# Delta-rule attention and an MLP mixer on one core: 180 steps of a written order of issue moved

## The chip, the cores and the metric

The kernel runs on one core of one Trainium2 chip. A core has five engines that take their instructions in order, each from its own queue: TensorE (PE in the profile), VectorE (DVE), ScalarE (ACT), GpSimd (POOL) and SyncE (SP), which here issues all the DMA transfers. The metric is the device time of one execution in microseconds (us); less is better.

## The reference

Two blocks follow each other. Each of 4 batches and 8 heads runs a delta rule over 768 positions with a 48x48 state, and the joined heads (768 rows of 384) pass a token mixer and a channel mixer:

```python
for t in range(S):                       # S = 768, per batch and head
    kt, vt, bt = k_n[:, :, t], v[:, :, t], beta[:, :, t, None]     # k_n: k over its norm
    y[:, :, t] = einsum('bhd,bhde->bhe', q[:, :, t], state)
    v_old = einsum('bhde,bhd->bhe', state, kt)
    state = state + bt * einsum('bhd,bhe->bhde', kt, vt - v_old)
xt = x.transpose(0, 2, 1)                # x: y with the heads side by side
h = maximum(xt @ w_tok1, 0) @ w_tok2     # 768 -> 256 -> 768
u = x + h.transpose(0, 2, 1)
out = u + maximum(u @ w_ch1, 0) @ w_ch2  # 384 -> 1536 -> 384
```

## The kernel before

The recurrence is computed in chunks. All work is cut into jobs, Python generators in which each `next` issues one step. A string, `order`, names the job whose next step is issued; the launch loop walks through it:

```python
for word in order.split():
    name, _, n = word.partition("*")
    for _ in range(int(n or 1)):
        next(jobs[name])
```

Nothing is reordered after that: each engine runs its instructions in this order, and waits for what an instruction needs. So the string sets, for each queue, what stands behind what. In all there are 2610 steps. The jobs, by letter, with the lines that matter:

- `w0` to `w33` load and round pieces of the weights: a DMA of 384 KB or 256 KB (L280), two ACT steps (L286, L287), a shift on DVE (L289), an addition on POOL (L293).
- `k` loads keys and queries of a unit (128 rows of one batch's chunk pair), `p` prepares it: squares on ACT (L539), norms on DVE and ACT, transposes on PE (L562, L582) with ACT copies, the scaled mask `mb` (L574, on POOL from the fourth unit on) and scaled keys (L592). `c` and `d` form gram matrices on PE (L511) and mask them into `gm` on DVE (L517).
- `t` hands quarters of a unit's `gm` to an inversion: for the first six units by copies on ACT (L674), DVE (L677) and POOL (L679), later by four DMA writes to `n_dram` (L686). `i` inverts for several units at once, a chain on DVE: a transpose (L731) or a read of `n_dram` (L733), then for each row a product (L747) and an addition (L751); in the early rounds, at the end, a transpose (L757), an ACT and a DVE scaling (L758, L759). `f` brings the parts back (for later rounds by DMA from `w_dram`, L711).
- `h` (first six units only) and `j` join the inverted parts: PE products `p_z` (L781) and `p_x` (L794, L888), ACT copies (L799). The first `h` also fills a tile `z` with zeros on POOL (L619).
- `r` is the recurrence: `r0` to `r23` for the first two batches, `r24` to `r35` for the last two together, a serial chain through PE (L1013, L1038, L1042, L1056, L1059), DVE (L1022, L1070) and ACT (L1047, L1076, L1081), with a DMA of the output rows (L1083) and `l` to read them back (L1095).
- `m0`, `m1` are the mixers of the first two batches; `T2` is the token part of the third (L1227, six groups of PE matmuls, one per chunk, then L1242), `T3` of the fourth; `A`, `F`, `B` are the channel parts of the last two; `W`, `S`, `s` are sums of weights for them.
- `x`, `z` and `Y` issue matmuls on zeros whose result nobody reads (128x128 and 128x512 columns at L235, 64x128 at L245).

`order` begins with the weights, keys and warm matmuls, passes the six early units (inversion rounds 0 and 1), the writes of the third round's units, and from there mixes the recurrence with `m0` and `m1`. The line of `order` with `w22*4 t9*3` and the lines with `r34` and `T2` are those that the third and fourth places below belong to.

Of the kernel before, what the change touches and what calls it, by code (L numbers as in the profile page):

```python
# [23 lines left out]
def kernel(  # L24
# [1761 lines left out]
    h0 h1 h0 w8*2 h1 Y i0 f0 Y p4 f1 h2*2 p5*3 f0*2 w6 h0*5 k6*5 p6 z f2*2 k8*3 p5
    w6 p5 p3 p5 j0*3 f1*2 h1*5 j0*2 w8*2 w17 f2 h2*3 v0 t4*2 w17 r0*5 p6 h2*2 c5*2
    v1 w11*2 j1 p5 k7*2 c5 k7 c5 r0 c5 r0*2 w14*2 v1 w11*2 k7*2 p7 d5*5 r1*5 w14*2
    p6*2 t5 j1 t5*2 r1*2 j1 j2 p7 h3*2 r1*3 p6*3 i1*2 r2*5 k8*2 f3*2 w9 k9*3 j1*2
    v2*2 i1*3 j2*2 r2*2 f3 i1*2 p6*3 w16 v2 w16*3 r2*2 h3 r2 i1 d6 r3*5 i1*2 w9*3  # L1790
    v2 d6 h3 v2 w0 h3*2 r3 h3 d6*2 w0 d6 j3 c6*5 r3*4 w0 j2 w0 p8*2 j2 r4 p8 r4*4
    k9*3 j3*2 r4*2 i1*2 w24 i1*2 p7*7 r4 c7 r4 r5*5 k10 p9 k10 p9 c7 r4 c7*3 i1
    w5*2 p7 r5*2 w24*3 r5*3 j3*2 i1 r6*4 w26 v3*5 p9 k11 r6 d7*5 w26*3 p8*3 t6*2
    r6*2 w5*2 p8*4 v4*2 t6 i1 r6*3 h5*2 h4*2 k10*2 f4*3 c8*2 k10 p10 w28*2 c8*2 r7
    c8 r7*3 d8*4 p9 d8 w28 h4*5 p9 t6 r7*2 j4 w28 p9*3 r7*2 p9 w7 d9 w7 v4*2 f5*2
    w27*2 w7*2 d9*4 c9*2 f5 c9*3 t7*2 t8 r7*2 t7*2 j4*2 v4 p10*2 h5 r8*3 w29 t8*3
    w29 w27*2 r8*2 w29*2 q3 w29 j4*2 r8 w22*4 t9*3 r8*3 p9 r9 p10 r9*3 t9 v5 h5*3
    j5 i2 r9 w4*2 r8 h5 i2*5 w4 i2 w19*2 k10 w32 p10*2 w32 v7 k12 m0*2 k11 k12 q0
    v5*3 p10*2 r9*2 j5*2 k11*3 i2*2 r9 w4 i2 j5 i2*3 p10 v5 r9*2 d10*3 r10 v7*2 j5
    i2*2 r10*4 w12 i2 k12 i2*2 m0 w32 k11 k12 w32 r10*2 m0 p11 k12*4 w19 p11 r10  # L1800
    c10 r10 c10 r10 w33 d10*2 q2 Y r11*4 v7 r11*3 w19 c10 q1 w30 c10 r11 k12*2
    i2*3 r11 v6*4 i2*5 m0*3 i2*5 q5 i2 m0 p11*4 c10 p11 m0 p11*2 m0*2 k12*2 w12
    m0*3 v6 f6*3 w12 d11 c11*2 d11*2 c11 w33 c11 d11*2 j6 p12 w12 m0 w33 w30*3
    p12*2 f7*3 j6*2 m0 c11 j7 f6 f8 w27*2 f8 j7 f8 w15 f7 m0 w29 w33 w29 j7 r12*4
    w31 j8 p11 t10*3 r12 Y r12 f9 j8 f9 w21 p12 r12 f8 r13*2 w15*2 r12 w15 r13*3
    w31*3 Y r13*2 w33 j8 w21 m0 r13 q4 p12*4 r13*2 m0*2 r14 c12 f9 j9 r14*2 w21
    t10 w20*2 v7 r14*2 c12*2 w33 c12 r14 v8 c12*2 r14*2 w25*2 j9 r14 r15 v8 w21
    r14 r15 w25 r15*3 w25 k13*4 w20 k13*4 p13 k13*2 w20 v8*3 m0*2 p13 w25 p13 m0
    r15 p13 r15 p13 w27 w25 k13*2 j9 m0*4 p13 f9 w23 t12*3 p13 t12 w25 r15*3 c13*6
    w23 k14*7 r16*5 m0 p13 m0*3 w23*4 k14 r16*2 t11 t13*2 j9*2 t11*3 w33 p14 r16*2  # L1810
    p14*2 w31 m0*3 w31 m0 w31 m0 w23 r17*2 r16 t13 r17 t13 r17*2 p14*2 m0*2 p14 i3
    k14*4 i3*3 k15 v9*2 m0*3 v10 i3*5 k15 i3 r17 k15*2 p14 k15*3 m0 v10*2 i3 k15*2
    m0*2 k15*2 i3*4 r17*4 k15 i3*2 p14 m0*2 i3*6 m0*4 r18 i3 r18*2 v9*3 r18*2 i3*8
# [73 lines left out]
```

## Time and profile before

| what | us |
|---|---|
| median of three runs | 623.53 (623.19 to 623.9) |
| the profiled execution, its own time | 626.48 |
| span of its trace | 624.7 |
| PE busy | 594.3 |
| DVE busy | 466.1 |
| ACT busy | 256.6 |
| POOL busy | 110.2 |
| mean granted clock of PE | 0.973 of full |

A row of the timeline gives start, length, engine, line, operation, output<-input with shapes, the count, and in brackets the idle time of the engine ahead of it and what ended it. A stretch row gives the length, the busy us of PE, PEld, DVE, ACT and POOL, the granted PE clock, the DMA share and GB/s. The chain of work lists start, length and what held the end up. In the page, a digit is the share of a slice of 15.6 us in tenths.

### The profile page before, as it was taken

The page shows a single profiled execution, that of the slowest core. Times are in us where ns is not written, and L with a number is a line of the kernel's source. Part 1 is how long each engine was busy: PE and PEld are TensorE (multiplying, and loading weights), DVE is VectorE, ACT ScalarE, POOL GpSimd, SP SyncE. Part 2 cuts the span into 40 slices and gives each one's busy share as a digit, 9 for nine tenths or more (in the row PEclk, how much of TensorE's full clock was granted, in tenths as well). Part 3 has the DMA queues.
Part 4 walks back from the last instruction along what each step waited for, and adds up shares of the span by engine and source line. Part 5 has one row for each costly group of instructions (what it writes and reads, how often), then busy time and mean ns, then how long its engine had stood idle before and what let it go on. Part 6 is the DMA issues. An engine that isn't in the chain of part 4 may idle for free.

```text
span 624.7 us, 20909 instructions
## 1 busy us (share of the span) xinstructions
PE 594.3 (95%) x8733; PEld 519.7 (83%) x8733; DVE 466.1 (75%) x1160; ACT 256.6 (41%) x682; POOL 110.2 (18%) x150
## 2 busy tenths in 40 slices
PE   8489898899999999999999999999999999999998
PEld 5467776667898988977888888896699999999997
DVE  4986876986889845697567986866688898675874
ACT  7748787448522344213551305423252241404200
POOL 2346355215311121003020130011000000000000
PEclk9978897999999999999999999998999999999999
DMA  9566567657653244554544443134102012020001
GB/s 220 125 140 146 143 151 192 137 139 177 129 113 71 64 103 91 102 116 96 104 74 123 93 88 76 35 80 120 32 2 39 1 17 48 14 52 13 14 26 50
DMA packets 154605, 55.52 MB, mean 89 GB/s; under 512 B 129648, under 2 KB 148976, under 8 KB 154512
## 3 DMA queue, kind: packets, MB, share of 16 engines
q1 hardware_dynamic: 154512, 54.20, 38.3%
q8 instruction: 68, 1.11, 0.8%
q14 instruction: 25, 0.20, 0.1%
HBM read 41.19 MB, written 11.21 MB: 84 GB/s over the span
## 4 chain that ended last, share of the span: by engine, by line
PE 74%; DVE 10%; DMA 4%; ACT 3%; issue 2%; SPq 2%; POOL 0%; ACTq 0%; DVEq 0%
PE p_c L1672 13%; PE p_r L1502 13%; PE p_o L1693 10%; PE p_a L1574 6%; PE p_b L1574 6%; PE p_g L511 3%; PE p_h L1612 3%; DVE x L751 2%; PE p L1597 2%; DVE sub L747 2%; PE p_k L924 1%; DMA x<-n_dram 1%; PE p_h L1242 1%; PE p_s L962 1%; PE p_y L1038 1%
## 5 line engine op out<-in xcount | busy, mean ns | idle before, releaser
L1672 PE MATMUL p_c<-u_t,wc 128*128 128x256 f32 x432 | 101.6, 386 | 0.6 <-issue 0.6
L1672 PEld LDWEIGHTS p_c<-u_t,wc 128*128 128x128 f32 x432 | 79.6, 190 | 11.9 <-issue 1.1
L1693 PE MATMUL p_o<-wc,r 128*128 128x192 f32 x360 | 64.6, 331 | 0.7 <-DVE xb L1632 0.7
L751 DVE TENSOR_TENSOR x<-x,sub 128x84 f32<-128x84 f32 (+24 forms) x178 | 59.6, 335 | 6.1
L747 DVE TENSOR_TENSOR sub<-x 128x84 f32<-128x84 f32 (+24 forms) x178 | 57.7, 324 | 8.1 <-DMA x<-n_dram 3.5
L1693 PEld LDWEIGHTS p_o<-wc,r 128*128 128x128 f32 x360 | 58.4, 190 | 2.3 <-DVE xb L1632 1.3
L1681 ACT ACTIVATE r<-p_c 128x512 f32<-128x512 f32 x36 | 21.5, 596 | 49.3 <-PE p_c L1672 43.9
L511 PE MATMUL p_g<-kq 48*64 48x128 f32 (+1 forms) x704 | 35.2, 288 | 3.0 <-ACT kq L587 3.0
L517 DVE TENSOR_TENSOR gm<-p_g,mb 128x512 f32<-128x512 f32 x44 | 28.9, 684 | 9.5 <-PE p_g L511 8.4
L484 POOL TENSOR_TENSOR v_st<-v_st,nrm 128x384 f32<-128x384 f32 x12 | 11.2, 931 | 132.4 <-DMA v_st<-in_v_dram 104.8
L511 PEld LDWEIGHTS p_g<-kq 48*64 48x64 f32 (+1 forms) x704 | 27.1, 141 | 7.9 <-ACT kq L587 4.0
L574 POOL TENSOR_TENSOR mb<-mask_c,cs 128x512 f32<-128x512 f32 x20 | 21.2, 1061 | 65.3 <-DVE cs L552 35.7
L293 POOL TENSOR_TENSOR wc<-w_f,d 128x384 uint32<-128x384 uint32 x24 | 24.6, 1030 | 43.3 <-DVE w_f L289 20.2
L1502 PE MATMUL p_r<-t_d,wc 128*128 128x192 f32 x160 | 28.8, 326 | 0.0
L1515 DVE TENSOR_TENSOR kq<-kq,p_r 128x384 f32<-128x384 f32 x40 | 21.1, 552 | 10.2 <-PE p_r L1502 8.3
L1515 DVE TENSOR_TENSOR gm<-gm,p_r 128x384 f32<-128x384 f32 x40 | 21.2, 552 | 8.1 <-PE p_r L1502 5.8
L400 DVE STREAM_TRANSPOSE kq<-pads 128x512 f32<-128x512 f32 x24 | 25.6, 1109 | 1.6 <-DMA pads<-in_k_dram 1.2
L1502 PEld LDWEIGHTS p_r<-t_d,wc 128*128 128x128 f32 x160 | 26.5, 190 | 0.0
L1693 PE MATMUL p_o<-wc,s 128*128 128x192 f32 x144 | 25.7, 330 | 0.7 <-DVE xb L1632 0.7
L1502 PE MATMUL p_r<-pads,wc 128*128 128x192 f32 x128 | 25.4, 326 | 0.0
L1693 PEld LDWEIGHTS p_o<-wc,s 128*128 128x128 f32 x144 | 23.3, 190 | 1.3 <-DVE xb L1632 1.0
L1632 DVE TENSOR_TENSOR xb<-xb,p_o 128x192 f32<-128x192 f32 x42 | 14.7, 349 | 12.7 <-PE p_o L1693 12.3
(315 smaller groups left out, 1390.6 us busy)
## 6 DMA issues: line engine op xcount, KB each, us to landing
d<-in_moe_w_ch_dram SPq DMA_DIRECT2D x24, 384.0 KB, 3.9
v_st<-in_v_dram SPq DMA_DIRECT2D x96, 48.0 KB, 2.7
out_dram<-xb SPq DMA_DIRECT2D x23, 192.0 KB, 2.1
kst<-in_k_dram SPq DMA_DIRECT2D x64, 48.0 KB, 2.6
n_dram<-gm SPq DMA_DIRECT2D x72, 32.0 KB, 2.4
pads<-in_k_dram SPq DMA_DIRECT2D x24, 96.0 KB, 3.0
pads<-in_q_dram SPq DMA_DIRECT2D x24, 96.0 KB, 2.7
gm<-w_dram SPq DMA_DIRECT2D x72, 32.0 KB, 2.1
```

The source lines that it names most:

```text
L293: nc.gpsimd.tensor_tensor(out=dst.bitcast(U32), in0=f, in1=lo, op=ALU.add)
L400: nc.vector.transpose(kq_of[p // 2][:, i, :, p % 2].rearrange("f p (s g) -> f p g s", g=G), rows_of[i].rearrange("s p (g d) -> s p g d", g ...
L511: nc.tensor.matmul(p_g[PAR[i ^ cc ^ swap(u)], p], kqt[f, p, cc, 0], kqt[f, p, cc])
L517: nc.vector.tensor_tensor(out=blocks(gm_of(u))[:, :, cc, D:GW].rearrange("s p (two n) -> s p two n", two=2), in0=p_g, in1=made[u][:, :, cc ...
L747: nc.vector.tensor_tensor(out=tmp, in0=by[0].to_broadcast(list(to.shape)), in1=by[1].to_broadcast(list(to.shape)), op=ALU.mult,)
L751: nc.vector.tensor_tensor(out=to, in0=to, in1=tmp, op=ALU.add)
L1502: nc.tensor.matmul(p[:, i], pieces[q // width][:, at : at + 128], f[f"u{n}"], start=first and i == 0, stop=True, skip_group_check=True,)
L1515: nc.vector.tensor_tensor(out=o, in0=o, in1=p, op=op_of(sign))
L1574: nc.tensor.matmul(p, a[:, i], w[:, i // 2, i % 2], start=first and i == 0, stop=True, skip_group_check=True,)
L1672: nc.tensor.matmul(p_c[:, k], piece_of(wc1, cb, f * 128)[:, f * 128 : (f + 1) * 128], u_t[:, cb], start=(cb == 0), stop=(cb == NCB - 1),)
L1681: nc.scalar.activation(r2[:, m], p_c, ACTF.Relu)
L1693: nc.tensor.matmul(p, a[:, m], wc2[:, m, j], start=(start and i == 0), stop=(i == NM - 1), skip_group_check=True,)
```

## The change

180 of the 2610 steps stand elsewhere in `order`, none by more than 120 places; all others keep their order. No step is added or removed. Its table of words says little to a reader, so here is one line of each side from the start, and what it does to the queues after that:

```diff
-    w10 x*4 z w10*2 z w1*4 k1*3 z k1*3 z b p1 z p1 k0*6 p0*2 b*2 p1 w2 p0*5 p1*2
+    w1*4 k1 w10 k1 x k1 x k1 z k1 w10 k1 w10 z*3 k0 b k0 p1 k0 z k0 p1 k0*2 p0*2
```

In the start, two of four `x` go behind the beta step, the DMA of weight piece `w3` goes behind the third unit's loads, and its ACT, DVE and POOL steps go from the front of the queues to the neighbourhood of inversion round 0 (`w3`'s shift on DVE now directly ahead of L731). `w2`'s shift goes ahead. Inside round 0, the shift of `w13` goes from near the end of the chain to behind its first row. The square (L539) of the seventh unit goes on ACT from behind the copies of the first `h` (L799) to behind the third `h`'s last products.

On POOL around round 0 (names: `w_117`, `wc_119` are weights, `mb` the masks of a unit, `z` the zeroed tile, `r_124` what the inversion reads and writes; the third and fourth L293 from the top are w2's and w3's, or w2's alone, L293 with `d_282` and `d_275` is w18's, with `d_403` and `d_397` w13's). Before:

```order
L293 TENSOR_TENSOR w_117<-w_f,d_207 128x256
L679 COPY r_124<-wc_120 32x8x32 x2
L679 COPY r_124<-gm 32x8x32 x2
L293 TENSOR_TENSOR wc_119<-w_f,d_282 128x384
L574 TENSOR_TENSOR mb<-mask_c,cs 128x512
L293 TENSOR_TENSOR wc_119<-w_f,d_403 128x384
L652 MEMSET r_124 128x32x16
L619 MEMSET z_571 128x2304
L592 TENSOR_TENSOR gm<-kst_98,cs 128x8x48
```

and now:

```order
L679 COPY r_124<-wc_120 32x8x32 x2
L679 COPY r_124<-gm 32x8x32 x2
L293 TENSOR_TENSOR w_117<-w_f,d_349 128x256
L293 TENSOR_TENSOR wc_119<-w_f,d_275 128x384
L574 TENSOR_TENSOR mb<-mask_c,cs 128x512
L293 TENSOR_TENSOR wc_119<-w_f,d_397 128x384
L619 MEMSET z_582 128x2304
L592 TENSOR_TENSOR gm<-kst_98,cs 128x8x48
L652 MEMSET r_124 128x32x16
```

w3's addition comes behind the copies, and the zeroing and the scaled keys go ahead of the small memset L652, which waits for the end of round 0.

On PE around the first `h`, from the transposes of the fifth unit (`pads`) on: the four L235 of 128x512 ahead of its L562 and the one behind it come, before, as one and two around its last gram matmuls; the `Y` matmuls (L245) stand between the two groups of `p_z`. Before:

```order
L562 MATMUL p_t<-ident,pads 128x128 x4
L582 MATMUL p_t<-ident,pads 128x128 x4
L511 MATMUL p_g<-kq 64x128 x12
L235 MATMUL p_warm<-warm 128x128
L235 MATMUL p_warm<-warm 128x512
L511 MATMUL p_g<-kq 64x128 x4
L235 MATMUL p_warm<-warm 128x512 x2
L781 MATMUL p_z<-r_124,wc_120 64x32 x32
L245 MATMUL p_warm<-warm 64x128 x8
L781 MATMUL p_z<-r_124,gm 64x32 x16
```

and now:

```order
L235 MATMUL p_warm<-warm 128x512 x4
L235 MATMUL p_warm<-warm 128x128 x2
L562 MATMUL p_t<-ident,pads 128x128 x4
L235 MATMUL p_warm<-warm 128x512
L582 MATMUL p_t<-ident,pads 128x128 x4
L511 MATMUL p_g<-kq 64x128 x12
L245 MATMUL p_warm<-warm 64x128 x8
L235 MATMUL p_warm<-warm 128x128
L511 MATMUL p_g<-kq 64x128 x4
L781 MATMUL p_z<-r_124,wc_120 64x32 x32
L781 MATMUL p_z<-r_124,gm 64x32 x16
```

The `Y` matmuls go ahead of the last gram matmuls, so that the `p_z` groups follow each other, and nothing is left on PE between those gram matmuls and the first `p_z`.

On SP ahead of the read for inversion round 2 (`d_…` is the target of a weight load). Before:

```order
L686 DMA n_dram<-gm 32x8x32 x3
L303 DMA wc_dram<-wc_120 128x192
L280 DMA d_1875<-in_moe_w_ch_dram 128x384
L686 DMA n_dram<-gm 32x8x32 x4
L444 DMA v_st<-in_v_dram 64x4x48
L733 DMA x<-n_dram 128x1024
```

and now:

```order
L686 DMA n_dram<-gm 32x8x32 x3
L303 DMA wc_dram<-wc_120 128x192
L686 DMA n_dram<-gm 32x8x32 x4
L280 DMA d_1916<-in_moe_w_ch_dram 128x384
L444 DMA v_st<-in_v_dram 64x4x48
L733 DMA x<-n_dram 128x1024
```

The 384 KB of weights go behind the last four writes of the round's units.

On PE at the end of the recurrences (`p_k`, `p_y`, `p_w`, `p_s` belong to `r34`, `p_x` to a join, the pair of L1227 to one step of `T2`). Before, from the end of the join ahead of it:

```order
L850 MATMUL p_z<-gm,zst 32x32
L1227 MATMUL p_6646<-xb,w_117 128x384
L1227 MATMUL p_6647<-xb,w_117 128x384
L1227 MATMUL p_6646<-xb,w_117 128x384
L1227 MATMUL p_6647<-xb,w_117 128x384
L1013 MATMUL p_k<-ss_t,kq 64x48 x2
```

and now, from the end of `r34`'s first four steps:

```order
L1013 MATMUL p_k_6668<-ss_t,kq 64x48 x2
L1227 MATMUL p_6685<-xb,w_117 128x384
L1227 MATMUL p_6686<-xb,w_117 128x384
L888 MATMUL p_x<-gm,zst 32x32 x16
L1038 MATMUL p_y<-ss_t,kq 64x48
```

The first two steps of `T2`, together ahead of `r34` before, stand behind its first four steps and behind its `p_w` matmuls; the third stands ahead of `r35` (before: between `p_w` and `p_s` of `r34`), the fourth between `r35`'s `p_k` and `p_y` (before: behind its `p_w`). On SP, one more write of `v_st` and the last `gm<-w_dram` of that join go ahead of the last store of `m1`.

The rest are moves by a few places in the stretch where the recurrence and the mixers share PE, among them the last of four n_dram writes of one unit in rounds 3 and 5, which go to the end, next to the read.

More of the change, by code (lines that the diff above doesn't have):

```diff
@@ L1786 @@
[L1786 to L1791, printed above, removed]
```

136 lines of the change are left out of this document (73 added, 63 removed).

## The prediction

> **What bounds the kernel now.** I read the page first: the busy line, the slices of PE and of its granted clock.
>
> ```profile
> PE 594.3 (95%) x8733; PEld 519.7 (83%) x8733; DVE 466.1 (75%) x1160; ACT 256.6 (41%) x682; POOL 110.2 (18%) x150
> ...
> PE   8489898899999999999999999999999999999998
> ...
> PEclk9978897999999999999999999998999999999999
> ```
>
> PE is busy for 95% of 624.7 us, and the digits below 9 stand at the left end and at one place two thirds through. So a change of order can win only there: the other stretches are matmuls back to back. The busy times by stretch say how much:
>
> ```profile
> 40.00:60.00 20.00, 17.35 (x442) 15.99 (x444) 13.17 (x24) 15.15 (x43) 12.11 (x17) 0.83 0.66 144
> ...
> 100.00:120.00 20.00, 16.78 (x293) 11.99 (x290) 14.72 (x44) 10.56 (x29) 6.17 (x8) 0.74 0.72 177
> ...
> 420.00:440.00 20.00, 18.72 (x479) 13.48 (x474) 13.97 (x29) 8.80 (x29) 1.60 (x1) 0.83 0.38 104
> 440.00:480.00 40.00, 40.00 (x218) 35.18 (x217) 30.81 (x71) 15.86 (x35) 0.00 (x0) 1.00 0.12 23
> ```
>
> The columns after the length are the busy us of PE, PEld, DVE, ACT, POOL, and then the granted clock. From 440 on PE has no idle time at all (40.00 of 40): what reaches 440 earlier ends earlier, us for us. Ahead of 120 PE waits for chains over DVE, ACT and DMA, and between 420 and 440 it loses twice, 1.28 us idle and a clock of 0.83. Those two places make up my sum. Elsewhere I cost the moved steps at nothing: their cover is PE's own queue, full there, and a step that came a few places late under it would first have to outlast the matmuls ahead of it. That bound is weakest for the third round's last write to n_dram and its like, which now go last on SP ahead of the read that needs them; I allow 0.6 us either way for all of these together.
>
> **The start, to the first inversion (round 0).** The chain into the inversion's first transpose, and the w3 rounding on ACT that leaves the front of the queue:
>
> ```profile
> 13.09 0.45 ACT L286 ACTIVATE d<-d 128x256 f32<-128x256 f32 x1
> 13.43 0.43 ACT L287 ACTIVATE d<-d 128x256 uint32<-128x256 uint32 x1
> ...
> 25.82 0.63 ACT L674 COPY r<-gm 128x256 f32<-128x256 f32 x1 [0.65 <-DVE gm L517]
> ...
> 27.39 1.25 DVE L731 STREAM_TRANSPOSE x<-r 128x1024 f32<-128x1024 f32 x1
> ```
>
> ACT rows follow each other almost without a gap from 9 to 24 us, so taking the pair out (13.09 to 13.43 + 0.43 = 13.86, 0.77 us) moves all behind it up. The pair comes back in the 0.65 us that ACT waits at 25.82, which covers it but for 0.1. Two fewer 128x128 warm-up matmuls stand ahead of beta, which PE starts when they are through; two steps of the 128x512 kind take 1.98 in a row below, so two of a quarter their width about 0.4. w3's DVE shift, now directly ahead of L731, costs 0.3, two thirds of its ACT instruction's 0.45, with the same 256 columns. −0.77 + 0.1 − 0.4 + 0.3 is **−0.8**, and I take −0.9 with w2's shift, which DVE now does earlier in a wait. Ends: −1.4 and −0.3 (DVE, not ACT, may turn out to set the pace).
>
> **Round 0 on DVE against POOL.** POOL instructions and the DVE ones they met:
>
> ```profile
> 27.44 1.01 POOL L293 TENSOR_TENSOR wc<-w_f,d 128x384 uint32<-128x384 uint32 x1
> 28.41 1.04 POOL L574 TENSOR_TENSOR mb<-mask_c,cs 128x512 f32<-128x512 f32 x1
> ...
> 38.48 2.01 POOL L619 MEMSET z<- 128x2304 f32 x1
> 40.46 0.99 POOL L592 TENSOR_TENSOR gm<-kst,cs 128x384 f32<-128x384 f32 x1
> ```
> ```profile
> 28.67 0.84 DVE L747 TENSOR_TENSOR sub<-x 128x28 f32<-128x28 f32 x1
> ...
> 36.79 0.18 DVE L747 TENSOR_TENSOR sub<-x 128x28 f32<-128x28 f32 x1
> ...
> 39.40 1.37 DVE L759 TENSOR_SCALAR r<-r,even 128x512 f32<-128x512 f32 x1 [0.79 <-ACT r L758]
> ...
> 85.19 0.48 DVE L759 TENSOR_SCALAR r<-r,even 128x512 f32<-128x512 f32 x1 [0.79 <-ACT r L758]
> ```
>
> The same 128x28 subtraction took 0.84 us under L574 and 0.18 without it: one two-input POOL instruction costs the chain 0.66. L759 took 1.37 under the memset against 0.48 in the next round: 0.89. Before, one such POOL instruction falls into the chain of subtractions. After, w3's and w18's L293 push L574 back, w13's L293 comes from the end of the round to its start, and the memset and L592 follow at once, all while the subtractions run. That is three more: 3 × 0.66 = +2.0, less the 0.89 at L759: **+1.1**. Ends: −0.9 (they slip between) and +3.1 (the memset holds DVE too, its 2.01 us). No row here shows a subtraction beside a memset.
> The Trainium skill ("SBUF — State Buffer", Practical consequences) says that a DVE instruction with two SBUF inputs and a GpSimd instruction that reads SBUF lock each other out for whole instructions, and that one which only writes does not. The 0.84 against 0.18 agrees with the first half; by the second the memset is free there, as in my middle value.
>
> **h0 to h2: warm-up off the chain, and a colder PE.**
>
> ```profile
> 37.46 1.98 PE L235 MATMUL p_warm<-warm 128*128 128x512 f32 x4
> 41.51 2.21 PE L781 MATMUL p_z<-r,wc 64*64 64x32 f32 x64 [2.06 <-DVE gm L517]
> 43.46 2.01 PE L245 MATMUL p_warm<-warm 64*64 64x128 f32 x16
> 45.20 1.79 PE L781 MATMUL p_z<-r,gm 64*64 64x32 f32 x32
> ```
>
> The 64x128 warm-up (L245) stood in the chain between h1 and h2, 43.46 to 45.20; it goes ahead of d4's last matmuls, where PE waits anyway: −1.74. But four 128x512 warm-ups leave the wait ahead of h0 too. Instead of 2.06 us PE then idles about 5 ahead of 41.5. In this trace the 2.06 already was followed by half clock (p_z took 1.79 for 32 here, against 2.21 for 64). If h0 and h1 run at half clock throughout, +2.2; if not at all, 0. I take +1.2, so **−0.5**; ends −1.7 and +0.5 for this stretch alone.
> The Trainium skill ("TensorE: Matmul & The Clock Gate", the table of what matters for kernels) advises against PE-idle gaps over about 3 us. By it the 5 us gap would certainly cost the clock, and this term would be +0.5; it speaks against this part of the change, and the trace, with a drop after 2 us, is stricter still.
>
> **The square of the seventh unit off ACT's path.** It stood between h0's copies and the next copy on ACT and goes behind h2's matmuls:
>
> ```profile
> 49.62 0.52 ACT L539 ACTIVATE ksq<-lent 128x384 f32<-128x384 f32 x1
> ```
>
> **−0.5**; ends −0.5 and 0 (ACT is then late for the step that wants it).
>
> **SP: 384 KB of weights behind the four n_dram writes.**
>
> ```profile
> 97.32 0.35 SPq L280 DMA_DIRECT2D d<-in_moe_w_ch_dram  x1
> 97.87 1.80 SPq L686 DMA_DIRECT2D n_dram<-gm  x4
> ```
> ```profile
> 99.22 3.75 DMA n_dram<-gm
> ...
> 103.12 3.94 DMA x<-n_dram
> ```
> ```profile
> n_dram<-gm SPq DMA_DIRECT2D x72, 32.0 KB, 2.4
> ```
>
> The last write lands 3.75 us after issue, against a median of 2.4, and round 2 on DVE waits for it and for the 3.94 of the read. With the weights behind, the write may be as fast as the median: −1.35. The first write waits for gm, which DVE ends only just before 97.87, so the issue itself gains nothing. The weights now meet the read instead and can give some back: **−0.9**; ends −1.35 and +0.5.
>
> **The end of the recurrences, 422 to 441.** The chain there:
>
> ```profile
> 420.65 5.19 DMA gm<-w_dram
> ...
> 427.69 1.49 PE p L1227 x4
> ...
> 429.55 0.43 issue
> ...
> 430.58 0.05 PE p_s L1056 x2
> ...
> 431.08 0.35 DVE ss_t L1070
> ...
> 432.26 0.37 DVE rw_t L1022
> ...
> 433.03 0.09 PE p_w L1042
> ...
> 434.62 2.86 PE p L1227 x4
> 437.48 1.50 PE p_y L1059 x32
> ```
>
> Steps r34 and r35 go from PE to DVE or ACT and back; PE waits 0.43, 0.35 and 0.37 us and little pauses more, about 1.2 together. Then the clock halves: the same L1227 group takes 2.86 instead of 1.49, the small matmuls come each 0.09 instead of 0.05. That is 1.4, some 0.9 for the 32 of p_y and p_w, and 0.7 in the 1.50: 3.0 us. After the change the first L1227 step goes behind r34's first four, the second behind r34's output, the third ahead of r35, the fourth into r35's own wait. Each group (1.49) is longer than the wait that it fills, so those waits go, and with them, I think, the low clock: −1.2 − 3.0. Against that: r35's later wait, which the fourth group filled, lies open, +0.7 (an estimate: the longest of the three waits here, 0.43, and a hand-over to ACT and back), and p_x needs gm, which landed at 425.84 (420.65 + 5.19) and held p_x until then. PE now has one L1227 group less ahead of p_x and asks for gm up to 1.49 earlier; as its landing may move up by part of that, +1.0. Sum **−2.5**; ends −3.5 (the landing moves up) and 0 (the clock falls nevertheless, and the open waits balance).
>
> **The sum**: −0.9 + 1.1 − 0.5 − 0.5 − 0.9 − 2.5 = −4.2 us. The profiled execution took 626.48 (span 624.7); the sum makes it 622.3 and 620.5. The median of the three runs, 623.53, is 2.95 below it; from there I forecast **619.3**.
>
> **The rivals.**
> 1. *More than that*: the earlier read of round 2 also ends a window of half clock in 100 to 120 (0.74 there), and gm lands early. 16.78 us busy at 0.74 hide up to 4.4 us; a third of it and 1.0 at the end give 623.53 − 4.2 − 2.4, about 617. For it: PE waits there for the same read. Against: nothing fills the wait itself.
> 2. *The end gives nothing*: gm<-w_dram (5.19 against the median of its kind, below) sets the pace, with a v load now ahead of it on SP; PE idles before p_x and the clock falls as before. 623.53 − 1.7 = 621.8, and with round 0 at its dear end (+3.1 for +1.1) 623.8.
>
> ```profile
> gm<-w_dram SPq DMA_DIRECT2D x72, 32.0 KB, 2.1
> ```
>
> 3. *Slower, by the cold PE*: the gap ahead of h0 brings half clock, and the chain of short matmuls behind it never fills a window, so it stays. 17.35 us busy at 0.83 would be 28.8 at 0.5, some +6 on the chain with half of it covered: 623.53 − 4.2 + 6 + 0.5 is about 626. The clock of 0.83 means (1 − 0.83) / 0.5 × 20 = 6.8 us at half there now; it decides if this grows by more than about 8. Against it: in the page's slices the clock has a dip and is back at 9 or 8 in the next one, and never stays low with matmuls of this kind behind each other.
> 4. *DVE held by the memset too* (+2.0 in round 0) gives 621.3; still faster, so it only widens.
>
> **How the numbers follow.** Forecast 0.55, first rival 0.15, second 0.16, third 0.14. Anything within 0.2% (1.25 us, about what a measurement of this kernel can tell) counts as the same: the second rival's dear half and a mild form of the third. So faster 0.74, same 0.13, slower 0.13. The range takes the first rival's 617 less its own 1.5 for the low end, 615.5, and for the high end the second's dear 623.8.
>
> **What would show it.** L731 starts at about 26.5; the subtractions of round 0 show three or four of 0.7 to 0.9; no L245 between the two p_z groups; a landing of n_dram below 3 us after its issue; round 2's first subtraction, released at 103.12 + 3.94 = 107.06 before, some 2.5 us earlier; full clock from 422 to 440, and L1227 at 1.5 in all its groups; the shift at 441 as large as at the end. I am wrong if the granted clock is low for longer ahead of 60, if p_x at the end waits for gm, or if the gain by 120 is not kept to 420, where I cost all at nothing.

## The result, and the profile after

The change makes the kernel slower. Beside each other on one chip, the median went from 623.36 us (4 runs, 622.22 to 623.9) to 629.94 us (4 runs, 627.83 to 633.21), a ratio of 1.011 [1.0071 to 1.0149]. A second comparison, with more runs, gave 626.98 against 622.17 us, 1.0092 [1.0066 to 1.0117]. I had forecast 619.3.

The profiled execution after took 627.83 us (span 626.1). Its page, busy line and the slices of PE and of its clock:

```profile
PE 589.9 (94%) x8733; PEld 516.1 (82%) x8733; DVE 471.2 (75%) x1160; ACT 257.2 (41%) x682; POOL 109.4 (17%) x150
...
PE   8768887898999999999999999998999999999998
...
PEclk9969999799999999999999999998999999999999
```

PE is 4.4 us less busy, and the span is 1.4 longer: PE waits more. The two traces lie closer than the kernels do. This execution is the fastest of its four, and its mean clock of 0.981 is 24 us at half clock; the profile of the kernel before, slower than its median, has 0.973, which is 34 us. The medians lie 6.6 us apart. The same stretches as in the prediction, now of the changed kernel, with two that I had not looked at:

```profile
40.00:60.00 20.00, 16.53 (x430) 15.12 (x432) 12.77 (x24) 15.88 (x46) 10.61 (x15) 0.77 0.51 107
...
100.00:120.00 20.00, 15.56 (x289) 11.30 (x289) 16.27 (x45) 10.64 (x28) 6.72 (x8) 0.83 0.71 187
120.00:160.00 40.00, 36.16 (x657) 25.99 (x655) 30.95 (x76) 21.91 (x61) 14.24 (x16) 1.00 0.62 149
160.00:400.00 240.00, 236.99 (x3940) 205.14 (x3932) 178.80 (x459) 83.44 (x243) 38.59 (x51) 1.00 0.43 93
...
420.00:440.00 20.00, 17.59 (x543) 12.70 (x542) 10.49 (x25) 7.85 (x25) 0.84 (x1) 0.91 0.49 124
```

And of the kernel before, the two that the prediction does not show:

```profile
120.00:160.00 40.00, 38.53 (x742) 28.47 (x741) 30.50 (x81) 23.31 (x64) 14.84 (x17) 1.00 0.61 145
160.00:400.00 240.00, 237.52 (x3975) 205.13 (x3973) 179.41 (x463) 83.74 (x244) 38.63 (x52) 1.00 0.43 94
```

From 120 to 160 PE is idle for 3.84 us instead of 1.47, in a stretch where I had costed every move at nothing. From 420 to 440 it is idle for 2.41 instead of 1.28, in the stretch that was to bring most of the gain. Step by step, the changed kernel stands against the kernel before like this (start of the same step in both traces; minus is earlier):

| step | before | after | difference |
|---|---|---|---|
| round 0's transpose, L731 | 27.39 | 26.37 | −1.02 |
| first p_z of h0 | 41.51 | 41.53 | +0.02 |
| round 2's first subtraction | 107.09 | 106.51 | −0.58 |
| r10's first step on PE | 116.90 | 114.52 | −2.38 |
| r11's first step on PE | 122.50 | 122.15 | −0.35 |
| m0's nineteenth step | 151.99 | 154.21 | +2.22 |
| m1's second step | 273.34 | 276.18 | +2.84 |
| T2's fifth step (L1227) | 438.90 | 440.66 | +1.76 |

Some of these differences are draws and not the change: they differ from one execution of the same kernel to the next. All runs of the kernel before, 151 over the comparisons below, spread from 617 to 629 us (standard deviation 2.5), and about half of such scatter goes with how much of the run PE spends at half clock. One execution shows one draw of that; so below, the ratios decide what a part is worth, and the traces what happens. A place is read best over all of the nineteen traces (before, after and the seventeen kernels below) that have the same order there.

### The profile page after: what moved, and what is told of

Read it like the earlier page. It is cut to its first block, busy times and chain, and to the rows that moved or that the text cites. A ratio compares the mean times of both kernels' runs of the same rounds, so it can differ in the third digit from the quotient of the medians.

```text
span 626.1 us, 20913 instructions
## 1 busy us (share of the span) xinstructions
PE 589.9 (94%) x8733; PEld 516.1 (82%) x8733; DVE 471.2 (75%) x1160; ACT 257.2 (41%) x682; POOL 109.4 (17%) x150
## 4 chain that ended last, share of the span: by engine, by line
PE 66%; DVE 10%; DMA 3%; issue 2%; SPq 2%; ACT 1%; DVEq 0%; ACTq 0%
PE p_r L1502 13%; PE p_c L1672 12%; PE p_o L1693 10%; PE p_a L1574 7%; PE p_b L1574 6%; DVE x L751 3%; DVE sub L747 3%; PE p_h L1612 2%; PE p_g L511 1%; DMA x<-n_dram 1%; PE p_y L1038 1%; PE p_h L1242 1%; PE p L1597 1%; PE p L1227 1%; PE p_h L1376 1%
## 5 line engine op out<-in xcount | busy, mean ns | idle before, releaser
L751 DVE TENSOR_TENSOR x<-x,sub 128x84 f32<-128x84 f32 (+24 forms) x178 | 63.5, 357 | 6.1
L747 DVE TENSOR_TENSOR sub<-x 128x84 f32<-128x84 f32 (+24 forms) x178 | 59.7, 335 | 6.9 <-DMA x<-n_dram 2.4
L293 POOL TENSOR_TENSOR wc<-w_f,d 128x384 uint32<-128x384 uint32 x24 | 24.7, 1033 | 39.4 <-ACT d L287 17.5
L1502 PEld LDWEIGHTS p_r<-t_d,wc 128*128 128x128 f32 x160 | 26.5, 190 | 0.0
```

Of the source, the lines that this page charges most:

```text
L293: nc.gpsimd.tensor_tensor(out=dst.bitcast(U32), in0=f, in1=lo, op=ALU.add)
L747: nc.vector.tensor_tensor(out=tmp, in0=by[0].to_broadcast(list(to.shape)), in1=by[1].to_broadcast(list(to.shape)), op=ALU.mult,)
L751: nc.vector.tensor_tensor(out=to, in0=to, in1=tmp, op=ALU.add)
L1502: nc.tensor.matmul(p[:, i], pieces[q // width][:, at : at + 128], f[f"u{n}"], start=first and i == 0, stop=True, skip_group_check=True,)
```

## The experiments

In most of them one cluster of the change is made alone, the rest of `order` as before. "Steps a to b" are places in `order`. Each was timed beside the kernel before in five rounds, several kernels to a chip; 12 runs each (after_again 6). The ratio is not the quotient of the two medians: for mid_only and tail_t2back they point opposite ways, which shows how little one such number tells. In a cut, the minus line is of the kernel that the entry starts from.

| kernel | median | before beside it | ratio, 95% interval |
|---|---|---|---|
| start_only | 623.69 | 622.61 | 1.0032 [1.0, 1.0064] |
| i2read_only | 623.62 | 622.61 | 1.0031 [0.9998, 1.0065] |
| mid_only | 622.28 | 622.61 | 1.002 [0.9991, 1.0049] |
| tail_only | 623.86 | 622.61 | 1.0024 [0.9993, 1.0055] |
| rest_only | 623.13 | 622.84 | 1.0017 [0.9988, 1.0046] |
| after_less | 625.68 | 622.84 | 1.0056 [1.0019, 1.0093] |
| after_again | 626.98 | 622.17 | 1.0092 [1.0066, 1.0117] |
| start_warm | 624.49 | 622.17 | 1.0049 [1.0018, 1.008] |
| start_pool | 623.99 | 622.84 | 1.0014 [0.9988, 1.0041] |
| front_only | 621.54 | 623.01 | 0.9968 [0.9938, 0.9997] |
| w22_only | 623.81 | 622.17 | 1.0019 [0.9985, 1.0053] |
| i2_nojp | 624.19 | 622.84 | 1.0046 [1.001, 1.0081] |
| i2_j5back | 624.39 | 623.01 | 1.0023 [0.9989, 1.0056] |
| w22_late | 626.83 | 624.48 | 1.0046 [1.0011, 1.0081] |
| tail_t2back | 621.83 | 622.17 | 1.0007 [0.998, 1.0033] |
| front_mid_t2back | 620.83 | 623.01 | 0.996 [0.9934, 0.9986] |
| best_w22 | 626.55 | 624.48 | 1.0031 [1.0001, 1.0062] |

### Where the loss sits: the change in pieces

**start_only** makes the change up to step 308 alone: the start, inversion round 0, h0 to h2 and the square.

```diff
-  i0*2 d4*2 k5 x z d4*3 c4 z*2 p5*2 k5 t4 p5 h0 h1 h0 w8*2 h1 Y i0 f0 Y p4 f1 h2*2
+  i0*2 d4*2 k5 Y*2 x d4*3 p5 w8 p5 w8 k5 p5 h0 c4 h1 h0 h1 i0 f0 p4 t4 f1 h2*2
```

> Before with only the first cluster of the change (first 307 steps: start, inversion round 0, h0 to h2, up to seventh unit's first loads). Theory P (places, from the two traces: start -1.0, POOL against round 0 +2.0, L759 -0.9, nothing left at 60 us): within 0.5 us of before. Rival C (the clock: the 5 us PE gap ahead of h0 gives two or three windows of half clock more, in most runs): 2 to 4 us slower than before, with a lower mean clock.

**i2read_only** changes steps 605 to 713: `w22`'s DMA goes behind the `n_dram` writes (t9), and r8, r9, j5, p10 and w4 move with it.

```diff
-  j4*2 r8 w22*4 t9*3 r8*3 p9 r9 p10 r9*3 t9 v5 h5*3 j5 i2 r9 w4*2 r8 h5 i2*5 w4 i2
+  q3 w29 t9*2 p9 p10*2 r9*2 t9 r9*2 t9 w22 v5 h5 w22 h5*2 r8 w22 j5 i2 w22 r9 w4*2 h5 i2*6
```

> Before with only the cluster around the read for inversion round 2 (w22 behind t9, r8, r9, j5, p10, w4). Theory P: 0.5 to 1.0 us faster, as the n_dram landing moves up. Rival C: the work that PE now does earlier (p10.5, m0.1) leaves a longer gap ahead of r9's end, half clock falls on m0 or r10; 0 to 2 us slower.

**mid_only** changes steps 724 to 1053: the later `Y`, p11, p12, t10 and t12.

```diff
-  d10*2 q2 Y r11*4 v7 r11*3 w19 c10
+  d10*2 q2 r11*4 v7 r11 p11 r11*2 w19 Y w19 c10
```

> Before with only the moves from round 2's 18th step to the fourteenth unit (Y, p11, p12, t10 against w31, t12). Theory P: 1 to 2 us slower, since the traces part by 2 us between 120 and 157. Rival C: within 0.5 us, since PE is full there and the clock does not fall; the parting comes from the earlier clusters.

**tail_only** changes steps 1998 to 2184, the end of the recurrences.

```diff
-  j23*2 T2 r33*2 T2 f23 r33 l s l s r33 j23 r34*4 j23 r34*2 W*3 v23*4 j23 r34*2 T2 r32 r34*5 r35*8 T2
+  j23*2 r33 l s*2 r33 j23 r33 r34*4 T2 r33 j23 r34*2 W*2 v23*2 l v23 j23 r34 T2 r34*5 T2 W r32 r34 r35*4 T2 r35*6
```

> Before with only the last cluster (T2 between the steps of r34 and r35, v23 and f23 on SP ahead of m1's last store). Theory P: 1 us faster (the lag falls from 2.85 to 1.75 there). My prediction said 2.5 us faster. Rival C: 1 us slower or more in most runs, with the half clock at 430 longer than before's two windows.

**rest_only** makes all that these four leave out: steps 311 to 611 and 1200 to 1950, mostly places of w, h, p, v and i between steps of r and m.

```diff
-  d7*5 w26*3 p8*3 t6*2 r6*2 w5*2 p8*4 v4*2 t6 i1 r6*3 h5*2 h4*2 k10*2
+  d7*2 w5 d7*2 t6 d7 w26 t6 w5 r6 w26 r6 w26 v4 p8 h4*2 v4 p8*2 t6 i1 r6*3 h5*2 k10*2
```

> Before with the moves not measured so far: between h2 and round 2 (w5, p8, w26, h4 and h5, k8) and after the fourteenth unit up to the tail (c15, c16, i4, v17, t18, t19, m1, i5). If the parts add up, this makes up what the four clusters leave of the whole: +0.5 to +2 us. Otherwise it is level, and the parts cost more together than alone.

**after_less** is the whole change without the clusters of i2read_only and tail_only.

```diff
-  q3 w29 t9*2 p9 p10*2 r9*2 t9 r9*2 t9 w22 ... j23*2 r33 l s*2 r33 j23 r33 r34*4 T2
+  j4*2 r8 w22*4 t9*3 r8*3 p9 r9 p10 ... j23*2 T2 r33*2 T2 f23 r33 l s l s r33 j23 r34*4
```

> The change without its cluster around round 2's read and without the tail cluster. If parts add up: 2.4 us below the change, about +2.5 over before. If only the tail and the read cost anything in truth, level with before.

**after_again** is the changed kernel as it is, without an edit.

> The changed kernel once more, beside the kernels below. If the loss adds up from places, the four clusters measured one by one (+1.7, +1.1, -0.1, +1.3 in the mean) leave it at +4 us over before, with 1.5 to 2.5 windows of half clock more. If it is a matter of luck in which window the gaps fall, the mean comes back to within 1.5 us of before.

What follows from these seven: no single cluster holds the loss. The five pieces give +0.32, +0.31, +0.20, +0.24 and +0.17%, together 1.24%, against 0.92 and 1.1 of the whole. Each of the five is uncertain by 0.3% and is at or near the edge of its interval, so this sum is no proof that parts add up. The loss itself is no draw: in its second set, after_again, the changed kernel did not come back to within 1.5 us of the kernel before. None of them brings the gain that I gave it: the terms up to step 308 −0.8 us, SP −0.9 and the end −2.5 became +2.0, +1.9 and +1.5 (the ratios times 622.6). And what I had costed at nothing, the other two pieces, takes its share, though no interval of its own excludes zero.

### The start and h0 to h2

**start_warm** is start_only with three 128x512 warm-up steps directly ahead of h0, to fill the gap that PE has there now.

```diff
-  p5 w8 k5 p5 h0 c4 h1
+  p5 w8 k5 p5 z*3 h0 c4 h1
```

> The start cluster with three more 128x512 warm-up matmuls directly ahead of h0, in PE's gap of 4.3 us. Theory C (the gap brings the half clock over h0 to h2, and that is what the cluster loses): the slow stretch from 39 to 49 us shrinks to one window or none, 1 to 2 us faster than the cluster alone, at or below before by up to 1 us. Rival P (POOL against round 0 takes the gain, the clock matters little there): unchanged against the cluster alone, within 0.5 us.

**start_pool** is start_only with POOL's work at round 0 as before: w13 back near the end, and L652 ahead of L619.

```diff
-  i0 w3 i0 w13*2 p4*2 ... c4*3 w13 w6*2 ... p5 h0 c4 h1 h0 h1 i0 f0 p4 t4 f1
+  i0 w3 i0 w13 p4*2 ... c4*3 w13*2 w6*2 ... p5 c4 t4 h0 h1 h0 h1 i0 f0 p4 f1
```

> The start cluster with POOL as before at round 0: w13's shift and addition near the end of the round, the small memset ahead of the large one. Theory P: the chain of subtractions loses one 0.7 to 0.9 us stall instead of three; L759 costs 1.37 again; h0 starts 0.5 to 1.0 us earlier than in the cluster alone, and the mean is 0.5 to 1 us lower. Rival C: h0 earlier, but the mean stays 1 to 2 us over before, since the windows of half clock stay at 9.4 on average.

**front_only** keeps the change's order only as far as round 0's first transpose; `z`, `Y`, POOL's work and the square around h0 to h2 stand as before.

```diff
-  d4*2 k5 Y*2 x d4*3 p5 w8 p5 w8 k5 p5 h0 c4 h1 h0 h1 i0 f0 p4 t4 f1
+  d4*2 k5 x z d4*3 c4 z*2 p5*2 k5 t4 p5 h0 h1 h0 w8*2 h1 Y i0 f0 Y p4 f1
```

> Before with only the change's order up to round 0's first transpose; z, Y and POOL around h0 to h2 as before. Theory W (the start cluster loses by windows of half clock behind the gap ahead of h0, while its head gains 1.5 us at L731): windows as before, about 8 on average, L731 1.5 us earlier, 0.5 to 1.5 us faster than before. Rival P: w3 and w18 on POOL against the subtractions take it back, level within 0.5.

PE's rows around h0, first of the changed kernel, then of front_only, then of start_warm (in brackets the idle time ahead and what ended it):

```profile
41.53 3.63 PE L781 MATMUL p_z<-r,wc 64*64 64x32 f32 x64 [4.43 <-DVE gm L517]
44.94 1.93 PE L781 MATMUL p_z<-r,gm 64*64 64x32 f32 x32
46.80 1.11 PE L562 MATMUL p_t<-ident,pads 128*128 128x128 f32 x4
```
```profile
38.04 1.99 PE L235 MATMUL p_warm<-warm 128*128 128x512 f32 x4
40.95 2.06 PE L781 MATMUL p_z<-r,wc 64*64 64x32 f32 x64 [0.92 <-DVE gm L517]
42.81 1.10 PE L245 MATMUL p_warm<-warm 64*64 64x128 f32 x16
43.71 1.11 PE L781 MATMUL p_z<-r,gm 64*64 64x32 f32 x32
44.75 0.66 PE L562 MATMUL p_t<-ident,pads 128*128 128x128 f32 x4
```
```profile
41.15 2.09 PE L781 MATMUL p_z<-r,wc 64*64 64x32 f32 x64 [0.33 <-DVE gm L517]
...
48.59 1.06 PE L855 MATMUL p_z<-t,wc 32*32 32x32 f32 x32 [2.38 <-DVE t L817]
```

and the stretch from 38 to 62, first of the kernel before, then of the changed kernel, of start_only and of front_only:

```profile
38.00:62.00 24.00, 20.73 (x513) 18.18 (x512) 16.13 (x30) 18.21 (x51) 15.96 (x21) 0.86 0.65 136
```
```profile
38.00:62.00 24.00, 18.43 (x492) 16.86 (x492) 16.11 (x33) 18.26 (x51) 12.47 (x17) 0.79 0.53 109
```
```profile
38.00:62.00 24.00, 19.52 (x491) 18.13 (x492) 15.41 (x30) 18.17 (x51) 12.39 (x16) 0.72 0.53 118
```
```profile
38.00:62.00 24.00, 21.48 (x597) 18.35 (x594) 18.06 (x34) 19.97 (x56) 17.76 (x21) 0.93 0.64 141
```

With the gap of 4.43 us both p_z groups run at half clock: 3.63 and 1.93 against 2.06 and 1.11. So though `Y` no longer stands between them, the group behind h0 starts at 46.80, not at 44.75. In 24 us PE of start_only is granted 0.72 of its clock against 0.93 in front_only and 0.86 before, which is 13.4 against 3.4 and 6.7 us at half (1 minus the clock, over 0.5, times 24). This is no draw: the five traces with the change's order of PE around h0 (start_only, start_pool, after, after_again, after_less) have 0.59 to 0.79 there, the ten with the order before 0.85 to 0.98, front_only and the two built on it 0.93 to 0.99.

front_only is the only variant of the start with an interval below 1, 2.0 us faster than before; start_only is 2.0 slower, and what stands between them is the order around h0 to h2, POOL's work at round 0 included. By the times, start_pool does not separate POOL from PE: its interval lies mostly within that of start_only. Its trace does: with POOL's work as before, and L759 beside the memset back at 1.38 us, its clock from 38 to 62 is 0.72 as in start_only. So the low clock goes with the order of PE's work, and not of POOL's.

start_warm, in a trace that is the fastest of its 12 runs, keeps the clock over h0 (0.86 from 38 to 62), but PE waits 2.38 us for the third unit's transpose on DVE (L817) and the half clock comes behind that: it loses no less. Warm matmuls in one place move the cold place to the next wait.

### The weights ahead of round 2's read

**w22_only** moves only w22 behind the n_dram writes.

```diff
-  j4*2 r8 w22*4 t9*3 r8*3 ... r9*3 t9 v5 h5*3 j5 i2 r9
+  j4*2 r8 t9*3 r8*3 ... r9*3 t9 w22 v5 h5 w22 h5*2 w22 j5 i2 w22 r9
```

> Before with only the 384 KB of weights (w22) behind the four n_dram writes, nothing of r8, r9, j5, p10. Prediction's step: landing of n_dram 1 us sooner, 0.5 to 0.9 us faster in the mean, at most. Rival J (the cluster lost by j5 and p10 being early on PE): also faster or level, since they are left out; only if this alone is slower does the write order cost.

**i2_nojp** is i2read_only with j5 and p10 at their places before. One gram product (d10) then reads keys before their last copy (p10.9), so this kernel computes that part from other numbers.

```diff
-  t9*2 p9 p10*2 r9*2 t9 ... h5*2 r8 w22 j5 i2 w22 ... p10 j5 p10 j5 r9*2 k11*3
+  t9*2 p9 r9 p10 r9 t9 ... h5*2 j5 r8 w22 i2 w22 ... p10*2 r9*2 j5*2 k11*3
```

> The cluster around round 2's read with j5 and p10 back in before's places (w22, r8, r9 and w4 as in the change). Theory J (PE stands 2 to 3 us at j5's second step, whose DVE part is not ready, and 0.9 at p10's second transposes): both waits go and this is 1 us faster than the whole cluster, level with before. Rival R (the read of n_dram, now beside the weights, takes 5.5 instead of 3.9 us, and that is the loss): no better than the whole cluster, +1 us against before.

**i2_j5back** moves back j5 alone.

```diff
-  h5*2 r8 w22 j5 i2 w22 ... p10 j5 p10 j5 r9*2 k11*3
+  h5*2 j5 r8 w22 i2 w22 ... p10*2 r9*2 j5*2 k11*3
```

> The cluster around round 2's read with only j5's steps back in before's places; p10, w22, r8, r9 as in the change. Theory J: PE's 2 to 3 us wait at j5's second step goes and the mean falls from +1.1 to about 0. Rival R (the read beside the weights is slow, and the round's chain on DVE is what PE waits for next): the wait turns up at r9 or r10 instead, the mean stays at +1 to +2.

**w22_late** is the kernel before with w22 behind the read of round 2 too.

```diff
-  j4*2 r8 w22*4 t9*3 ... j5 i2 r9 w4*2 r8 h5 i2*5 w4 i2 w19*2
+  j4*2 r8 t9*3 ... j5 i2 w22 r9 w4*2 r8 h5 i2*4 w22 i2 w22 w4 i2 w22 w19*2
```

> Before with w22 behind the read of n_dram as well, its rounding steps ahead of w19's. Theory R (the write is slow behind the weights, the read is slow beside them): now the last write lands about 1.7 us after its issue and the read takes about 3.9, round 2 starts some 2 us earlier, 0.5 to 1.5 us faster. Rival: PE's dense stretch from 125 us on starts no earlier, as ACT waits for the later weights: level or slower.

The last write to n_dram and the read behind it, in the chain of work that ended last (start, time from issue to landing), of the changed kernel, of i2read_only and of tail_only, which has the order before here:

```profile
98.32 2.89 DMA n_dram<-gm
...
101.36 5.13 DMA x<-n_dram
```
```profile
98.73 1.66 DMA n_dram<-gm
100.52 5.56 DMA x<-n_dram
```
```profile
100.07 1.72 DMA n_dram<-gm
...
101.93 3.76 DMA x<-n_dram
```

Against the 3.75 us of the kernel before, the write lands sooner in the changed kernel and in i2read_only. But it does so in tail_only too, with the weights ahead of it. The 3.75 was one draw. In that execution SP issued its four writes in 1.80 us and the last one landed late; in nine of the other ten traces with this order SP took 2.7 to 3.4 us to issue them (tail_only 3.06, the changed kernel 3.01). What counts is the whole way from the issue of the first of the four writes to round 2's first subtraction:

| place of w22's DMA | traces | first write to read | read to subtraction | together |
|---|---|---|---|---|
| ahead of the writes | 11 | 4.2 to 5.4 | 3.5 to 4.5 | 8.0 to 9.2, mean 8.6 |
| between writes and read | 6 | 4.2 to 4.8 | 5.2 to 5.8 | 9.5 to 10.4, mean 9.9 |
| behind the read | 2 | 4.3 | 3.8 | 8.0 and 8.1 |

Beside the weights the read takes 1.7 us longer, and the writes ahead of it gain 0.4. The two first rows do not overlap: the move costs round 2 about 1.3 us. That fits the times. The four kernels with this move and not the rest of the change (w22_only, i2read_only, i2_nojp, i2_j5back) are all above 1, by 0.19 to 0.46%, though only i2_nojp's interval excludes 1.

In w22_late the weights come behind both. Its rows of DVE, ACT and PE:

```profile
105.31 0.19 DVE L747 TENSOR_TENSOR sub<-x 128x30 f32<-128x30 f32 x1 [1.21 <-DMA x<-n_dram]
...
110.80 0.56 DVE L289 TENSOR_SCALAR w_f<-d 128x384 uint32<-128x384 uint32 x2 [2.74 <-ACT d L286]
```
```profile
108.62 0.43 ACT L286 ACTIVATE d<-d 128x256 f32<-128x256 f32 x1 [6.11 <-DMA d<-in_moe_w_tok_dram]
...
109.27 0.64 ACT L976 ACTIVATE xb<-p_y 64x192 f32<-64x192 f32 x2
```
```profile
117.36 0.34 PE L962 MATMUL p_s<-rw_t,gm 64*64 64x48 f32 x1 [3.90 <-ACT rw_t L954]
```

Round 2 starts at 105.31, 1.78 earlier than in the trace before (107.09), and by the table some 0.5 of that is the move. But the next weights, w4's, now wait behind w22's, and their rounding on ACT (L286) stands in ACT's queue ahead of the recurrence's copy (L976). ACT waits 6.11 us, the weights' shift (L289) holds DVE for 2.74 in the middle of round 2, and PE waits 3.90 for r9. The kernel is 0.46% slower. From 100 to 120 PE is idle for 8.29 us here and for 5.81 in best_w22 below, against 1.5 to 4.9 in the other seventeen traces. So none of the three places tried for this DMA is free: its price is paid on the way to the read, by the read itself, or by the queue that rounds what comes behind it.

Is j5 a part of i2read_only's loss? PE waited 2.95 us for it in that trace. With that wait gone, i2_j5back is not shown to be faster (1.0023 against 1.0031), nor is i2_nojp (1.0046): in i2_j5back PE waits 1.8 us for r10's input and 1.7 for r9's instead, as rival R had it. Whether the cluster loses more than the slow read is open.

### The end of the recurrences

**tail_t2back** is tail_only with the first of T2's groups ahead of r34 again.

```diff
-  r33 j23 r33 r34*4 T2 r33 j23
+  r33 j23 r33 T2 r34*4 r33 j23
```

> The last cluster with the first T2 step ahead of r34's first products again, the other three as in the change. Theory S (the 1.7 us stall inside r34's products has no wait behind it; it comes where some eighty short matmuls follow each other, and one long group between j23's products and r34 hides it): the stall goes, 2 to 3 us faster than the cluster alone, so 1 to 2 us faster than before. Rival F (gm's late landing sets the pace): p_x waits instead, no gain against the cluster alone beyond 0.5.

PE's stretches of 3.4 us, cut where the half clock begins or could begin in each execution, first before, then after, then mid_only and front_only, whose end is as before:

```profile
428.97:432.38 3.41, 2.50 (x99) 1.95 (x98) 0.87 (x4) 1.30 (x4) 0.73 (x1) 1.00 0.04 11
432.38:435.80 3.42, 3.13 (x64) 2.63 (x65) 3.35 (x10) 0.48 (x1) 0.00 (x0) 0.50 0.15 34
```
```profile
424.80:428.21 3.41, 1.65 (x45) 1.19 (x36) 1.64 (x5) 2.71 (x10) 0.00 (x0) 1.00 0.85 234
428.21:431.63 3.42, 3.42 (x95) 2.28 (x93) 1.91 (x3) 1.02 (x4) 0.00 (x0) 0.50 0.44 112
```
```profile
426.45:429.86 3.41, 2.72 (x112) 1.98 (x114) 1.96 (x6) 1.30 (x4) 0.99 (x1) 1.00 0.29 102
429.86:433.27 3.41, 3.41 (x99) 2.49 (x92) 3.34 (x9) 0.81 (x3) 0.00 (x0) 1.00 0.14 34
```
```profile
426.50:429.92 3.42, 3.42 (x36) 1.74 (x40) 0.79 (x1) 0.45 (x1) 1.20 (x1) 0.50 0.32 107
```

and PE's waits between 418 and 441, of the changed kernel and of tail_t2back (total us, times, longest):

```profile
PE p_k L1013 <- issue: 1.8, 1, 1.8
PE p_y L1059 <- ACT rw_t L1047: 0.6, 1, 0.6
```
```profile
PE p_s L1056 <- issue: 1.4, 1, 1.4
```

Two things stand here. First, the half clock that I wanted to remove was a draw. Thirteen of the nineteen traces have the order before at this place. Three have half clock there (before and after_less two steps of 3.4 us, front_only one), and ten have none. From r33's ninth step to T2's fifth those three took 18.70, 19.34 and 17.06 us, the ten 14.66 to 16.49. Second, the changed end took 17.94, 17.61 and 17.21 (tail_only, after, after_again). All three have a pause of 1.3 to 1.8 us inside r34's p_k, where PE waited for nothing that this view shows (the end of the document has more on it), and one step of half clock right behind it. So the change brought the half clock that it was to remove.

With the T2 group back ahead of r34, three traces (tail_t2back, front_mid_t2back, best_w22) have full clock throughout and took 16.60, 15.37 and 15.17 us; in tail_t2back the pause at p_k is 0.3, and another of 1.4 stands at r34's p_s. tail_t2back runs level with before. The edit's own effect on the time, 0.17% between tail_only and tail_t2back, is not settled, since their intervals overlap.

### Putting the good parts together

**front_mid_t2back** joins front_only, mid_only and tail_t2back.

> That head, the moves between round 2 and the fourteenth unit, and the last cluster with its first T2 step back: the parts that were not slower alone. If parts add up: 1 to 2 us faster than before. Rival: within 0.5 of before, as each was within its interval.

It beats both kernels: 620.83 against 623.01 us, 0.996 [0.9934 to 0.9986], about 2.5 us. How much of it is more than front_only's 0.9968 can't be told from these intervals.

**best_w22** adds w22 behind the read, as in w22_late.

```diff
-  j4*2 r8 w22*4 t9*3 ... j5 i2 r9 w4*2
+  j4*2 r8 t9*3 ... j5 i2 w22 r9 w4*2
```

> The head, the middle moves and the tail with T2's first step back, and w22 behind the read. If w22 gains what theory R says, 0.5 to 1.5 us below the same without it, 2.5 to 3.5 below before. Rival: no further gain, 2 us below before.

It throws the gain away, 1.0031. That w22 behind the read costs was thus seen twice.

## Why the prediction was wrong, step by step

**The start (−0.9): right, and a little small.** L731 starts at 26.37 for 27.39 in the changed kernel, −1.02. Over the nineteen traces it starts at 25.8 to 26.5 with the new start and at 26.9 to 28.2 with the old one, 1.6 apart in the mean. The front alone, in front_only, is the one part that makes the kernel faster. (One term was 0.1 too small by its own row: two warm-ups of a quarter of 1.98 us are 0.5 and not 0.4.)

**Round 0 (+1.1): right, in kind and size.** DVE's rows of the changed kernel, then POOL's:

```profile
27.63 0.73 DVE L747 TENSOR_TENSOR sub<-x 128x28 f32<-128x28 f32 x1
28.40 0.96 DVE L751 TENSOR_TENSOR x<-x,sub 128x28 f32<-128x28 f32 x1
...
29.77 1.05 DVE L751 TENSOR_TENSOR x<-x,sub 128x52 f32<-128x52 f32 x1
30.85 0.23 DVE L747 TENSOR_TENSOR sub<-x 128x72 f32<-128x72 f32 x1
...
32.86 0.78 DVE L751 TENSOR_TENSOR x<-x,sub 128x108 f32<-128x108 f32 x1
...
40.30 0.49 DVE L759 TENSOR_SCALAR r<-r,even 128x512 f32<-128x512 f32 x1 [0.79 <-ACT r L758]
```
```profile
27.28 1.01 POOL L293 TENSOR_TENSOR wc<-w_f,d 128x384 uint32<-128x384 uint32 x1
28.25 1.04 POOL L574 TENSOR_TENSOR mb<-mask_c,cs 128x512 f32<-128x512 f32 x1
29.75 1.00 POOL L293 TENSOR_TENSOR wc<-w_f,d 128x384 uint32<-128x384 uint32 x1 [0.45 <-issue]
30.69 2.02 POOL L619 MEMSET z<- 128x2304 f32 x1
32.68 0.83 POOL L592 TENSOR_TENSOR gm<-kst,cs 128x384 f32<-128x384 f32 x1
```

Four instructions of DVE are long, each beside one of POOL's additions or products; those beside the memset keep 0.23 to 0.27; L759 falls from 1.37 to 0.49. From L731 to the first p_z the ten traces with the order before take 14.11 to 14.13 us, the five with the changed one 15.16 to 15.24. By 41.5 the start's gain of this pair is used up: the first p_z is at +0.02. The fourth rival, that the memset holds DVE, is out for the subtractions, and for them these rows agree with what the Trainium skill says ("SBUF — State Buffer", Practical consequences) of an instruction that only writes. L759 is another matter: before it ended at 40.77, 0.28 us after the memset (38.48 + 2.01 = 40.49), and in start_pool again 0.29 after it (39.91 and 39.62). It looks held until the memset is through: it took 1.34 to 1.38 us in all fourteen traces that have the memset there, and 0.48 or 0.49 in the five that have not. No run moved the memset alone.

**h0 to h2 (−0.5): wrong, and the largest mistake of the first half.** The mechanism was named, with its sign in the balance. The term that was too small is the cold PE: I priced it at +1.2 for two matmul groups and should have priced the stretch to 62, where the clock is 0.72 in start_only against 0.86 before. That is 6.7 us more at half clock and up to 3.3 us of matmul time. start_only and front_only differ by 0.64% (4 us; their intervals do not overlap). The third rival, slower by the cold PE, about 626, was nearest the truth: its cold PE came, though it did not stay for good. I let a growth of 8 us at half clock from 40 to 60 decide for it. In the profile after it was not reached: (1 − 0.77) / 0.5 × 20 is 9.2, 2.4 more than before. In the second execution, after_again, the clock there is 0.60, which is 16, 9 more; start_only has 0.68, 6 more.

**The square (−0.5): not seen.** It runs 6.56 us later (56.18 for 49.62); behind it nothing starts earlier that the traces could show apart from the clock.

**SP (−0.9): wrong in sign.** The step that failed is the price of the write. I took the 3.75 us of one execution for what the weights cost the write, and the other traces with that order show that it was not: all the way from the first write to the read there are 0.4 us to gain, not 1.35. What the weights cost the read is 1.7 us, where I had allowed 0.45.

**The end (−2.5): wrong, the largest single miss.** The step that failed is "the clock halves ... 3.0 us": I read a low clock in one profile as a property of the order, and ten of thirteen traces of that order do not have it. (The 0.9 inside it has no row to stand on either: the 0.05 us of its row is for two matmuls.) Without it the term is −1.2 + 0.7 + 1.0 = +0.5, and the new pause in r34, with the half clock behind it, makes it a loss: tail_only's 1.0024 is +1.5 us, with an interval from −0.4 to +3.4. The wait for ACT in r35, +0.7, came as said (0.6). The +1.0 for p_x did not come: it waits for gm in none of the six traces with T2 moved.

**All else at nothing: wrong.** The condition that I gave, "if the gain by 120 is not kept to 420", came true: the difference goes from −2.38 at r10 to +2.84 at m1's second step. PE's idle time from 120 to 160 tells it from a draw. It is 3.84 and 3.70 us in the two executions of the changed kernel, 2.1 to 2.6 in the five others with the moves of mid_only or rest_only, and 1.0 to 1.8 in the twelve without. So PE's queue was not the cover that I took it for. The rows of it that I can name are a weight piece's rounding on ACT that waits for its DMA, holding the recurrence's copy behind it,

```profile
147.75 0.54 ACT L286 ACTIVATE d<-d 128x384 f32<-128x384 f32 x1 [1.33 <-DMA d<-in_moe_w_ch_dram]
```

and PE's pauses of 0.94 us ahead of 148.08 and of 1.23 ahead of 153.60, of the kind told at the end. But mid_only has this wait too (0.88) and is not shown to lose time, so it is not shown that these add up to the loss. after_less, with neither the SP cluster nor the end, loses 0.56%, so much of it comes from the start, the middle and the rest together.

The first rival (617) never came near. The second (621.8 to 623.8, the end gives nothing) had the right place but not the sign, and gm, which it made the cause, was not waited for.

## What to carry to other kernels

- A clock dip in one profile may be a draw. Before a forecast counts on removing it, it must be seen in further executions of the same order; here it was the largest term, and it stood in three of thirteen. The same holds for one slow landing of a DMA.
- A DMA, a warm-up or a weight's rounding that is moved off a chain lands on another queue. Ask what is next in that queue: w22 had a price in each place that was tried.
- Where a chain of short steps leaves PE idle, ask what moving the warm-ups does to the clock behind it. Taking them out of the chain made it shorter and colder, and lost more than it gained.

## What I had not expected of the hardware

**Half clock comes in steps of 3.413 us, and after little idleness.** In the changed kernel it begins at 32.27, 39.09, 110.77 and 428.21, all multiples of 3.413 apart, and lasts one to three such steps. The Trainium skill ("TensorE: Matmul & The Clock Gate", Part 1) gives a free-running window of 3413 ns, and the steps agree; the same page's advice, to avoid gaps over about 3 us, does not cover these cases. A window with 1.76 us idle (1.65 of 3.41 busy, above) was followed by half clock, and so was one with 0.91 (before, 428.97), while one with 0.69 (mid_only, 426.45) and one with 1.39 (tail_t2back, 426.96 to 430.38) were not. In the nineteen traces half clock set in 93 times, always behind a window in which PE was busy for at most 3.06 us; but many windows with as little were not followed by it, so what else decides is open. Over all runs of these comparisons, a kernel's time rises by 1.3 us for each such window at half clock (an estimate, from a fit with one constant per kernel, residual 1.7 us); the kernel before has 8.0 of them on average, start_only 9.5, front_only 7.3. By that fit, start_only at equal windows would be level with before, and the changed kernel's second set still 2.5 us slower, a part that the clock does not explain.

**PE pauses at fixed counts of its matmuls, behind packets of instructions.** The pauses marked "issue" of 0.2 to 1.9 us fall at counts that are multiples of about 127 matmul records apart (after the 7336th in the changed kernel and the 7339th in tail_t2back, then the 7464th there, 125 on). The list of DMA queues on the changed kernel's page has this line (packets, MB, share):

```profile
q8 instruction: 69, 1.13, 0.8%
```

Each of the 69 packets has 16 KB. PE has 8733 matmuls and as many weight loads, which is 253 of them for each packet, or 127 matmuls with their loads. All 77 such pauses from 0.2 us up in the nineteen traces end 1.1 to 1.6 us after one of these packets has landed; the one in r34's p_k, at 427.14, ends 1.40 us after a landing at 425.74. This fits that PE stands there until its next instructions have come, though no run changed how they are supplied. Which step is hit depends on how many matmuls stand ahead of it, so an order can move a pause into a chain.
